# Three moves in the step plan of a linear-attention block: splits of the folded weight, one tile's statistics, one pair's feature maps

## The chip, the cores and the metric

The kernel runs on one core of a Trainium2 chip. The metric is the device time of one execution in microseconds; "before" is the median of three runs. The profile shows one execution of its own. The engines are named as the profile names them: PE (matmul; PEld is its weight load), DVE (VectorE), ACT (ScalarE), POOL (GpSimd) and SP, whose queue issues the transfers. Each works through its own instructions in the order in which the program issues them, and waits for others by semaphores.

## The reference

All numbers are 32-bit floats; S = 2048 rows, D = 576, H = 32 heads of 18, F = 4608.

```python
def _A_ref(x, wqkv, wo):
    qkv = (x @ wqkv).reshape(B, S, 3, H, Dh).transpose(2, 0, 3, 1, 4)
    q, k, v = qkv[0], qkv[1], qkv[2]
    phi = lambda t: jnp.where(t > 0, t + 1, jnp.exp(t)) + 1e-6
    pq, pk = phi(q), phi(k)
    kv = jnp.einsum("bhsd,bhse->bhde", pk, v)
    z = jnp.einsum("bhsd->bhd", pk)
    num = jnp.einsum("bhqd,bhde->bhqe", pq, kv)
    den = jnp.einsum("bhqd,bhd->bhq", pq, z)[..., None] + 1e-6
    o = num / den
    return o.transpose(0, 2, 1, 3).reshape(B, S, D) @ wo

xn = _layernorm(x)
s = _A_ref(xn, A_wqkv, A_wo)
g = _silu(gelu(xn @ w1 + b1) @ w2 + b2)
return x + s * g
```

## The kernel before, in words

Every matrix product is made from operands that are split in a high part (ACT casts it) and a low part (DVE or POOL subtracts), three matmuls for one. Most products also use a seven-product scheme on 2x2 blocks, so blocks of x and of the weights are added and subtracted first. There are three phases.

**Keys and values.** The 2048 rows are 16 tiles of 128, taken in eight pairs p = 0 to 7; `(p, s)` is tile s of pair p. Each tile is loaded (`load_x`, SP), its statistics are taken (`x_stats`, L237: five short instructions on DVE, then a power and a product on POOL), it is normalized on ACT (`x_norm`, L251), transposed by PE into the one PSUM tile `pt` (`transpose_x`, L266), and its parts are written (`x_hi`, `x_raw`, `x_lo`, `x_lo_tmp`, the block sums `x_sum` into `scr`, then `s_hi` on ACT and `s_lo`, L315, on DVE). `x_store` sends the parts to DRAM from SP's queue. Pair 0 is written out by hand (L530 to L586); for pairs 1 to 7 `plan_pair` (L600) puts calls into the table `plans` by step number, 14 steps (`NSP`) for a pair, and `at_step` issues a step's calls, in the order in which they were added, behind a piece of the pair's matmuls. Pair 1's keys are plain products (`Plain`); later pairs use `Proj`, whose second product `b` reads `xSL`, the low parts of the sums. The feature map of a key tile `ka` or `kb` is `phi_exp` (ACT), `phi_max` (L437, DVE) and `phi_add` (L440, ACT); the tiles then go into the state (`do_state`, PE, step 3 of the next pair) and into a running sum on POOL (`k_sum`). In pair 1 `wkq.sums` makes block sums of the key weight on POOL (L180), and `wkq.split_sums` splits them (L156 on ACT, L157 on DVE).

**Queries.** Rounds r = 0 to 9, again 14 steps each. Round 0 folds the attention state into the output weight (`fold_wo`, L771): PE writes 126-row blocks, which are copied to `kw`, and transfers from SP's queue (L794, L797) move their rows into tiles `kr` of 128 rows. `split_kw` (L767) makes the high part `kw_h` on ACT (L768) and the low part `kw_l` on DVE (L769) of one such tile. Splits 0 and 1 are issued in round 0 and at step 3 of round 1. In rounds 1 to 7 a `Proj` in the order `K_UP` = (1, 6, 7, 5, 2, 4, 3) makes the queries of a pair: product 1 goes to PSUM `a` and ACT copies it (L361); 6 and 7 are added up on DVE (L364, L367); 5 goes to `e`, and DVE adds it up (L357); 2 is accumulated onto `a`, which the copy must have read; 4 goes to `z` again, which L367 must have read; 3 is accumulated onto `e` behind L357. Behind it stand the exponentials and maxima of the queries, the denominators (`den_mul` POOL, `den_sum` DVE, `den_div` POOL), a padding copy on ACT (`pad`, L826), the transposes (`transpose_p`, `p_hi`, `p_lo`: L841, L845, L846) and from r = 2 on the attention product `Attend` (L866), which reads `kw_h` and `kw_l` of all five row blocks; `store` copies it from PSUM on ACT (L874).

**The gated feed-forward.** 18 steps over chunks of the hidden size, by a table of the same kind (`NS` = 28 steps each). `W2.hi` and `W2.lo` split the second weight's blocks; the first chunk's blocks are planned by `PW2` with one more entry.

What sets the order around the change is therefore the step number, and within a step the order of the `add` calls; all engines and SP's queue issue in that order.

Of the kernel before, what the change touches and what calls it, by code (L numbers as in the profile page):

```python
# [37 lines left out]
NSP = 14  # L38
# [4 lines left out]
def linear_attention_gated_ffn(ctx, tc, x, wqkv, wo, w1, b1, w2, b2, out):  # L43
    nc = tc.nc
# [91 lines left out]
    def pair_cols(p):  # L136
        return p % 4
# [99 lines left out]
    def x_stats(p, s, first=False):  # L237
        st = t1.tile([P, 2, 6], F32, tag="st", name=f"st{p}{s}")
        raw = xraw[p, s]
        nc.vector.bn_stats(st[:, 0, :], raw[:, :HD])  # L240
        nc.vector.bn_stats(st[:, 1, :], raw[:, HD:])
        mv = t1.tile([P, 4], F32, tag="mv", name=f"mv{p}{s}")
        nc.vector.bn_aggr(mv[:, 0:2], st)
        nc.vector.tensor_scalar_add(mv[:, 2:3], mv[:, 1:2], 1e-5)
        nc.gpsimd.tensor_tensor(mv[:, 3:4], mv[:, 2:3], nhalf, op=ALU.pow)
        if not first:
            nc.vector.tensor_scalar(mv[:, 0:1], mv[:, 0:1], -1.0, None, op0=MUL)
            nc.gpsimd.tensor_tensor(mv[:, 2:3], mv[:, 0:1], mv[:, 3:4], op=MUL)
        stats[p, s] = mv

    def x_norm(p, s, on_vector=False):  # L251
        mv, raw = stats.pop((p, s)), xraw.pop((p, s))
        t = xn[p, s] = t1.tile([P, 640], F32, tag="xn", name=f"xn{p}{s}")
        parts = (t[:, :D], raw), (t[:, D:], raw[:, 512:])
        if on_vector:
            for dst, src in parts:
                nc.vector.tensor_scalar(dst, src, mv[:, 0:1], mv[:, 3:4], op0=SUB, op1=MUL)
            return
        for dst, src in parts:
            nc.scalar.activation(dst, src, AF.Identity, scale=mv[:, 3:4], bias=mv[:, 2:3])  # L260
# [25 lines left out]
    def x_lo(p, s):  # L286
        cs, src = pair_cols(p), pts[p, s]
        tt = nc.vector.tensor_tensor
        if s == 0:
            tt(xL[:, 0:4, cs], src[:, :4], xH[:, 0:4, cs].bitcast(F32), op=SUB)  # L290
        else:
            tt(xL[:, 4:6, cs], src[:, 2:4], xH[:, 5:7, cs].bitcast(F32), op=SUB)
        r = xH[64:, 4 + 3 * s, cs]
        tt(r, src[64:, 4], r.bitcast(F32), op=SUB)
# [17 lines left out]
    def s_hi(p):  # L312
        nc.scalar.copy(xSH[:, :, pair_cols(p)], s_raw)

    def s_lo(p):  # L315
        cs = pair_cols(p)
        nc.vector.tensor_tensor(
            xSL[:, :, cs], s_raw[:, :8], xSH[:, :8, cs].bitcast(F32), op=SUB
        )
        r = xSH[64:, 8, cs]  # L320
        nc.vector.tensor_tensor(r, s_raw[64:, 8], r.bitcast(F32), op=SUB)

    def x_store(p):
        cs = pair_cols(p)
        for t, a, b in X_PARTS:
            nc.sync.dma_start(x_dram[p // 4][:, cs, a:b], t[:, :, cs].bitcast(F32))
# [180 lines left out]
    def add(step, fn, *args):  # L507
        plans.setdefault(step, []).append((fn, args))
# [64 lines left out]
    x_raw(1, 0)  # L573
    x_lo(1, 0)
    x_norm(1, 1)
    s_hi(0), s_lo(0)
    x_stats(2, 0)
    x_store(0)
    plain_v(0, 1).part(0, N14)
    phi_exp(k_t[1], e_t[1])  # L580
# [19 lines left out]
    def plan_pair(p):  # L600
        base = p * NSP
# [57 lines left out]
        ka, kb = k_ts[p % 2]  # L659
        ea, eb = e_t  # L660
        if p == 1:
            add(base + 3, phi_exp, ka, ea)
            add(base + 4, phi_max, ka, ea)
            add(base + 5, phi_add, ka)
            add(base + 11, k_sum, ka)
        else:
            add(base + 6, phi_exp, ka, ea)
            add(base + 7, phi_max, ka, ea)
            add(base + 7, phi_add, ka)
            add(base + 8, k_sum, ka)  # L670
        add(base + 7, phi_exp, kb, eb)
        add(base + 8, phi_max, kb, eb)
        add(base + 10, phi_add, kb)
        add(base + 12, k_sum, kb)
        for n, j in enumerate(W2_FIRST.get(p, ())):
            add(base + (1, 3)[n], w2_sum, j)
# [18 lines left out]
    for p in range(1, NPAIR):  # L695
        plan_pair(p)
        base = p * NSP
        if p > 1:
            pr = Proj(p, wkq, k_ts[p % 2], mu1)
            steps = [(pr.step, (i,)) for i in K_UP]  # L700
        else:
            pr = plain_k(p, 0)
            steps = [(pr.part, v) for v in ((0, 5), (5, 10), (10, 14))]
            steps += [(lambda a, b: cur.update(pr=plain_k(1, 1)) or cur["pr"].part(a, b), (0, 4))]
            steps += [(lambda a, b: cur["pr"].part(a, b), v) for v in ((4, 8), (8, 11), (11, 14))]
        for k, (fn, args) in enumerate(steps):
            fn(*args)
            at_step(base + k)
        for s in range(2):
            pr = plain_v(p, s)  # L710
            for k, v in enumerate(((0, 5), (5, 10), (10, 14))):
                pr.part(*v)
                at_step(base + 7 + 4 * s + k)
            if s == 0:
                at_step(base + 10)
# [18 lines left out]
    base = NPAIR * NSP  # L734
# [237 lines left out]
    for r in range(NPAIR + 2):  # L972
        base = (NPAIR + r) * NSP
# [20 lines left out]
        if 1 <= r < NPAIR:  # L994
            a, b = q_tiles(r)
            at = base + 2 * (r == 2)
# [4 lines left out]
            add(at + (8 if r > 1 else 14), phi_add, a)  # L1001
            add(at + (9 if r > 1 else 15), phi_add, b)
        if r == 1:
            add(base + 6, split_kw, 2, nc.vector)
            add(base + 8, split_kw, 3, nc.vector)
        if 1 <= r <= 6:
            add(base, w2_load, r + 2, *((w1p, "wa") if r % 2 == 0 else (w2rp, "w2raw")))
        if 2 <= r <= 7:
# [24 lines left out]
        if 1 <= r < NPAIR:  # L1033
            for s in range(2):
                at = Attend(r - 2, s) if r >= 2 else None
# [14 lines left out]
        elif r == NPAIR:  # L1050
            w = w1t[0]
            at = Attend(r - 2, 0)
# [6 lines left out]
            at = Attend(r - 2, 1)  # L1059
# [12 lines left out]
        elif r > NPAIR:  # L1072
            for s in range(2):
                at = Attend(r - 2, s)
# [328 lines left out]
    def plan_w1(add, w, base, T, hi, lo):  # L1403
        for table, what in ((T, w.T), (hi, w.hi), (lo, w.lo)):
            for i, at in table.items():
                add(base + at, what, i)
# [11 lines left out]


    PW2 = {1: 3, 7: 4, 3: 6}  # L1420
    W2_SUMS_NEXT = {5: 23, 6: 27}
    W2_SUMS_FIRST = {4: 4, 5: 6, 6: 10}
    W2_NEXT = {1: 15, 2: 17, 7: 19, 4: 21, 5: 23, 3: 25, 6: 27}
# [14 lines left out]
    w2t = {}  # L1438
# [5 lines left out]
    for step in range(n_chunks):  # L1444
        half, c = divmod(step, NC)
        base = step * NS
        plain = step == n_chunks - 1
        h = HOps(c)
        if half == 0:
            plan_w1(add, w1t[2 * step + 1], base, **P1)  # L1450
            if step == 0:
                add(base + 2, w2t[step].sum7)
            for i, at in PW2.items() if step else (*PW2.items(), (2, 5)):
                add(base + at, w2t[step].hi, i)
                add(base + at, w2t[step].lo, i)
            if step == 0:
                for i, at in W2_SUMS_FIRST.items():
                    add(at, w2t[0].load, i)
        if half == 0 and c < NC - 1:
# [11 lines left out]
            add(base + 25, nxt.lo, 4)  # L1471
            for i, at in W2_SUMS_NEXT.items():
                add(base + at, lambda i=i, n=step + 1: w2t[n].load(i))
# [102 lines left out]
```

## Time and profile before

| | |
|---|---|
| median of 3 runs | 1124.46 us (1124.1 to 1124.77) |
| the profiled execution | 1125.04 us, its span 1123.3 us |
| mean granted TensorE clock | 0.996 of full |
| PE busy | 1103.1 us, 98% of the span |
| DVE busy | 835.4 us, 74% |
| ACT busy | 506.4 us, 45% |
| POOL busy | 483.8 us, 43% |

The span is the time from the first to the last instruction of the one profiled execution; the times of the runs hold what lies around it too. Busy time is a mean over phases with different limits: PE's 98% come mostly from the feed-forward. In a row of the timeline stand start and duration in us, engine, line, operation, what is written and read, the shape, and in brackets the idle time of the engine just before and what ended it. In a row of waits stand the total in us, the number of waits and the longest. A row by stages has its start and end, its length, the busy time of PE, PEld, DVE, ACT and POOL with the number of instructions, the granted clock, the share of time in which the DMA engines were busy, and GB/s.

### The profile page before, as it was taken

Reading aid. Unit: us, or ns where it says so; the run is one execution under the profiler, and the core shown is the slowest. Engines: PE = TensorE matmul, PEld = TensorE weight load, DVE = VectorE, ACT = ScalarE, POOL = GpSimd, SP = SyncE. Lnnn points to the kernel's source line nnn. Section 1 sums busy time; section 2 is a strip of 40 time slices with the busy share of each in tenths; the row PEclk is TensorE's granted clock in tenths of the full one; section 3 lists DMA queues with packets and bytes.
Section 4 is the critical chain, followed back from the end, with each engine's and each line's share of the span. In section 5 each row is a group of like instructions: output and inputs, shape, how many; then the busy total and the mean of one; then the engine's idle time right before and its main releaser. Section 6 shows DMA issues by size and latency. Waiting matters only on the chain.

```text
span 1123.3 us, 18672 instructions
## 1 busy us (share of the span) xinstructions
PE 1103.1 (98%) x6924; PEld 1017.8 (91%) x6924; DVE 835.4 (74%) x1250; ACT 506.4 (45%) x913; POOL 483.8 (43%) x411
## 2 busy tenths in 40 slices
PE   8899998999999999999999999999999999999997
PEld 7899998999988988989989899898898998989987
DVE  5878766877598988989889898666475674764766
ACT  6756643555545454454544544524233242242352
POOL 5555334555364644646456444325234232242340
PEclk9999998999999999999999999999999999999999
DMA  5756536784978477485584849978666666766243
GB/s 201 270 210 240 222 99 203 259 295 153 352 280 332 144 274 263 167 321 179 231 295 159 319 157 366 390 249 266 221 199 222 210 207 209 230 200 222 87 130 125
DMA packets 89098, 257.16 MB, mean 229 GB/s; under 512 B 9581, under 2 KB 20333, under 8 KB 86959
## 3 DMA queue, kind: packets, MB, share of 16 engines
q1 hardware_dynamic: 89007, 255.96, 64.5%
q8 instruction: 55, 0.90, 0.3%
q14 instruction: 36, 0.29, 0.1%
HBM read 155.03 MB, written 100.01 MB: 227 GB/s over the span
## 4 chain that ended last, share of the span: by engine, by line
PE 81%; DVE 8%; ACT 4%; issue 3%; DMA 2%; POOL 2%; SPq 0%; DVEq 0%; POOLq 0%; ACTq 0%
PE pm L1255 32%; PE e L1118 11%; PE zy L1118 10%; PE a L1118 10%; PE b L1118 4%; PE pl L404 4%; PE ps_s L866 2%; PE pd L1372 2%; PE e L349 1%; DVE w2o L501 1%; PE z L349 1%; DMA kr<-kw 1%; DVE h_l L896 1%; PE ps_kva L457 1%; PE a L349 1%
## 5 line engine op out<-in xcount | busy, mean ns | idle before, releaser
L1262 DVE TENSOR_TENSOR macc<-pm,macc 128x576 f32<-128x576 f32 x218 | 164.1, 753 | 47.9 <-PE pm L1255 46.7
L893 ACT CAST h_h<-g 128x512 fp32r<-128x512 f32 x204 | 120.0, 621 | 142.2 <-PE pm L1255 141.1
L896 DVE TENSOR_TENSOR h_l<-g,h_h 128x512 fp32r<-128x512 f32 x204 | 171.3, 840 | 0.0
L1223 POOL TENSOR_TENSOR mid<-g 128x512 f32<-128x512 f32 x34 | 44.0, 1295 | 185.0 <-ACT g L1126 185.0
L1118 PE MATMUL a<-xH,wa 128*128 128x512 f32 x360 | 117.1, 390 | 0.0
L1118 PEld LDWEIGHTS a<-xH,wa 128*128 128x128 f32 x360 | 67.6, 188 | 13.6
L1126 ACT ACTIVATE g<-b,b1c 128x512 f32<-128x512 f32 x36 | 24.8, 690 | 121.5 <-DVE b L1144 121.5
L1118 PE MATMUL e<-xSH,wb 128*128 128x512 f32 x216 | 66.7, 390 | 0.9 <-DVE b L1144 0.9
L1343 POOL TENSOR_TENSOR fin1l<-fin1h,fin1l 128x288 f32<-128x288 f32 x8 | 6.5, 807 | 121.5 <-DMA fin1l<-s_dram 64.7
L1217 POOL TENSOR_TENSOR g<-g 128x512 f32<-128x512 f32 x34 | 49.5, 1457 | 20.8 <-DVE h_l L896 19.5
L1135 ACT COPY mid<-a 128x512 f32<-128x512 f32 x36 | 21.2, 588 | 78.4 <-PE a L1118 78.3
L1118 PE MATMUL a<-xL,wa 128*128 128x512 f32 x144 | 56.2, 391 | 0.0
L1220 POOL TENSOR_TENSOR g<-g 128x512 f32<-128x512 f32 x34 | 49.9, 1469 | 13.1 <-DVE h_l L896 11.7
L1214 POOL TENSOR_TENSOR g<-g 128x512 f32<-128x512 f32 x34 | 51.3, 1508 | 2.7
L1138 DVE TENSOR_TENSOR mid<-b,mid 128x512 f32<-128x512 f32 x36 | 24.6, 684 | 35.4 <-PE b L1118 35.3
L1118 PE MATMUL b<-xSH,w 128*128 128x512 f32 x144 | 50.2, 389 | 0.0
L1118 PE MATMUL zy<-xSH,w 128*128 128x512 f32 x144 | 50.2, 389 | 0.0
L1118 PE MATMUL e<-xSH,w 128*128 128x512 f32 x144 | 50.2, 389 | 0.0
L1118 PE MATMUL zy<-xH,w 128*128 128x512 f32 x144 | 50.2, 389 | 0.0
L1118 PEld LDWEIGHTS e<-xSH,wb 128*128 128x128 f32 x216 | 40.6, 188 | 10.1 <-DVE b L1144 1.8
L896 DVE TENSOR_TENSOR h_l<-mid,h_h 128x512 fp32r<-128x512 f32 x34 | 43.1, 1268 | 6.0 <-ACT h_h L893 6.0
L1126 ACT ACTIVATE g<-e,b1c 128x512 f32<-128x512 f32 x36 | 24.8, 690 | 48.8 <-DVE e L1151 48.8
(928 smaller groups left out, 3589.2 us busy)
## 6 DMA issues: line engine op xcount, KB each, us to landing
op<-w SPq DMA_DIRECT2D x72, 256.0 KB
w<-op SPq DMA_DIRECT2D x72, 256.0 KB
w1raw<-w SPq DMA_DIRECT2D x18, 640.0 KB
w2raw<-w SPq DMA_DIRECT2D x10, 1152.0 KB
op_a<-wa SPq DMA_DIRECT2D x18, 640.0 KB
wa<-op_a SPq DMA_DIRECT2D x18, 640.0 KB
op<-w2o SPq DMA_DIRECT2D x19, 576.0 KB
w2r<-w SPq DMA_DIRECT2D x6, 1152.0 KB
```

The source lines that it names most:

```text
L349: nc.tensor.matmul(ps, st, mv, start=first and n == 0, stop=n == len(seq) - 1, skip_group_check=True,)
L404: nc.tensor.matmul(self.ps[n], st, self.wk(hl, k, n), start=(i == 0), stop=(i == n_all - 1))
L893: nc.scalar.copy(pair[0], src)
L896: eng.tensor_tensor(pair[1], src, pair[0].bitcast(F32), op=SUB)
L1118: nc.tensor.matmul(ps.rearrange("p (c j) -> p c j", c=4), st, mv, start=first and n == 0, stop=n == len(seq) - 1, skip_group_check=True,)
L1126: nc.scalar.activation(g, ps, AF.Gelu_apprx_tanh, bias=b1c[:, f : f + 1])
L1214: tt(src[5, pr], A(1, 0), A(1, 1), op=ADD)
L1217: tt(src[6, pr], src[5, pr], A(0, 0), op=SUB)
L1220: tt(src[3, pr], A(0, 1), src[6, pr], op=SUB)
L1223: tt(src[7, pr], A(0, 0), A(1, 0), op=SUB)
L1255: nc.tensor.matmul(ps[:, q, :HD], hs[p][st][:, cs], m[:, p, :], start=(n == 0 and i not in CHAIN), stop=(n == len(seq) - 1), skip_group_ch ...
L1262: nc.vector.tensor_tensor(dst, src, dst, op=ADD)
```

## The change

Three groups of calls are moved; no call is added or left out. The statistics of tile (2, 0), the fifth to be normalized, are issued ahead of `s_hi(0)` and `s_lo(0)`. In pair 1 the first key tile's `phi_max` goes from step 4 to 6 and its `phi_add` from 5 to 9; the second tile's `phi_add` from 10 to 11. In round 1 `split_kw(2)` goes from step 6 to 12, and `split_kw(3)` from step 8 to step 2 of round 2. The table `PW2_FIRST` holds the same entries as the expression that it replaces, and the calls stand at the same steps.

```diff
@@ -573,8 +573,8 @@
     x_norm(1, 1)
+    x_stats(2, 0)
     s_hi(0), s_lo(0)
-    x_stats(2, 0)
     x_store(0)
@@ -660,8 +660,8 @@
         if p == 1:
             add(base + 3, phi_exp, ka, ea)
-            add(base + 4, phi_max, ka, ea)
-            add(base + 5, phi_add, ka)
+            add(base + 6, phi_max, ka, ea)
+            add(base + 9, phi_add, ka)
             add(base + 11, k_sum, ka)
@@ -670,7 +670,7 @@
         add(base + 8, phi_max, kb, eb)
-        add(base + 10, phi_add, kb)
+        add(base + (11 if p == 1 else 10), phi_add, kb)
         add(base + 12, k_sum, kb)
@@ -1001,8 +1001,8 @@
         if r == 1:
-            add(base + 6, split_kw, 2, nc.vector)
-            add(base + 8, split_kw, 3, nc.vector)
+            add(base + 12, split_kw, 2, nc.vector)
+            add(base + NSP + 2, split_kw, 3, nc.vector)
@@ -1418,6 +1418,7 @@
     PW2 = {1: 3, 7: 4, 3: 6}
+    PW2_FIRST = {1: 3, 7: 4, 2: 5, 3: 6}
@@ -1448,11 +1449,12 @@
-            for i, at in PW2.items() if step else (*PW2.items(), (2, 5)):
-                add(base + at, w2t[step].hi, i)
-                add(base + at, w2t[step].lo, i)
+            w2c = w2t[step]
...
+            for i, at in (PW2 if step else PW2_FIRST).items():
+                add(base + at, w2c.hi, i)
+                add(base + at, w2c.lo, i)
```

More of the change, by code (lines that the diff above doesn't have):

```diff
@@ L1450, in linear_attention_gated_ffn @@
             plan_w1(add, w1t[2 * step + 1], base, **P1)
-            if step == 0:
-                add(base + 2, w2t[step].sum7)
-            for i, at in PW2.items() if step else (*PW2.items(), (2, 5)):
-                add(base + at, w2t[step].hi, i)
-                add(base + at, w2t[step].lo, i)
+            w2c = w2t[step]
+            if not step:
+                add(base + 2, w2c.sum7)
+            for i, at in (PW2 if step else PW2_FIRST).items():
+                add(base + at, w2c.hi, i)
+                add(base + at, w2c.lo, i)
             if step == 0:
```

## The prediction

> **What bounds the kernel now.** I read the page first: its span and the granted clock in 40 slices.
>
> ```profile
> span 1123.3 us, 18672 instructions
> ...
> PEclk9999998999999999999999999999999999999999
> ```
>
> The reader is to see that one slice of 28.1 us (the seventh, 168 to 197 us) ran below full clock, and that it is the slice in which the moved splits of the folded weight stand. Next, what TensorE waited for, over the whole span:
>
> ```profile
> PE a L349 <- ACT scr L361: 2.6, 1, 2.6
> ...
> PE pt L270 <- DVE scr L310: 1.6, 1, 1.6
> PE pt L270 <- ACT wkq_h L156: 1.3, 1, 1.3
> ```
>
> All three lie in the steps the change edits: the 2.6 us at r = 2 of the query rounds, the other two in pair p = 1. Third, the chain of work that ended last.
>
> ```profile
> 70.50 0.80 PE b L349 x4
> ...
> 161.05 1.06 PE a L349 x8
> ...
> 164.24 6.33 PE ps_kw L783 x24
> 170.93 11.43 DMA kr<-kw
> ```
>
> From 70.50 to 164.24 the chain has rows of PE alone, so whatever pair 1 wins or loses by 70 us arrives whole at 164 us. Then it follows a row transfer for 11.43 us, to 182.4 us. Fourth, ACT in order of time behind that transfer, and PE beside it.
>
> ```profile
> 182.44 0.67 ACT L768 CAST kw_h<-kr 128x576 fp32r<-128x576 f32 x1 [4.07 <-DMA kr<-kw]
> 183.01 0.77 ACT L435 ACTIVATE e<-scr,c 128x576 f32<-128x576 f32 x1
> ...
> 184.36 0.66 ACT L768 CAST kw_h<-kr 128x576 fp32r<-128x576 f32 x1
> 184.92 0.39 ACT L361 COPY scr<-a 128x288 f32<-128x288 f32 x1
> ```
>
> ```profile
> 182.50 0.29 PE L349 MATMUL e<-wkq_rl,xH 128*128 128x288 f32 x1
> 185.36 0.61 PE L349 MATMUL a<-wkq_h,xH 128*128 128x288 f32 x1 [2.57 <-ACT scr L361]
> ...
> 191.74 0.54 PE L866 MATMUL ps_s<-kw_h,th 128*128 128x288 f32 x2
> ```
>
> ACT runs its queue in order. It sits 4.07 us on split 2, whose rows are in flight; behind it wait two exponentials, split 3 and the copy of `a` (L361), and PE needs that copy before it may add onto `a`: 2.57 us without work. By stages, the clock:
>
> ```profile
> 31.50:35.00 3.50, 1.93 (x17) 1.73 (x16) 3.42 (x9) 1.89 (x3) 2.18 (x4) 1.00 1.01 346
> ...
> 181.70:185.10 3.40, 1.09 (x9) 0.85 (x7) 1.96 (x3) 2.66 (x5) 0.00 (x0) 1.00 0.35 96
> 185.10:188.50 3.40, 3.05 (x11) 2.71 (x12) 3.22 (x8) 2.65 (x5) 1.85 (x2) 0.51 0.98 406
> 188.50:192.00 3.50, 3.50 (x17) 3.50 (x16) 3.20 (x6) 0.24 (x1) 2.90 (x3) 0.50 1.02 411
> ```
>
> The first figures are PE's busy time, the third from the end the clock. Behind a stretch with PE busy 1.09 of 3.40 us the clock is half for 6.9 us; behind one with 1.93 of 3.50 (the 1.6 us wait above) it stays full. So the 2.57 us wait is paid twice.
>
> **Part 1: the query rounds.** Split 2 moves from step 6 to 12 of r = 1, split 3 to step 2 of r = 2. No instruction is added and no DMA is moved; the transfers start where they did, so I let split 2's rows land at 182.44. What is new is the order on ACT: the two exponentials (inputs ready, nothing else on ACT in the 4.07 us) now run inside the wait, then split 2, then the copy. The copy starts at 182.44 + 0.57 (the step from the split to the next start) = 183.01 instead of 184.92. PE's wait shrinks to about 183.45 - 182.79 = 0.7 us. The wait for the rows is not removed; two exponentials and split 3, 1.9 us, leave the path behind it. Queued behind split 2 are now the copy, a cast and two adds on ACT, and PE waits for the copy: each us by which the rows land later is lost one for one. Split 3 found its rows at 184.36 without a wait and asks for them at 185.2, behind the adds: no new wait. What is late next stands on DVE:
>
> ```profile
> 183.14 0.76 DVE L769 TENSOR_TENSOR kw_l<-kr,kw_h 128x576 fp32r<-128x576 f32 x1 [3.40 <-ACT kw_h L768]
> ...
> 185.83 0.45 DVE L364 TENSOR_TENSOR scr<-b,scr 128x288 f32<-128x288 f32 x1
> 186.20 0.68 DVE L845 TENSOR_TENSOR tl<-ptp,th 128x512 fp32r<-128x512 f32 x1
> ...
> 187.22 0.46 DVE L367 TENSOR_TENSOR scr<-z,scr 128x288 f32<-128x288 f32 x1
> 187.81 0.46 DVE L357 SCALAR_TENSOR_TENSOR rt<-e,scr 128x288 f32<-128x288 f32 x1
> ```
>
> The low part of split 2 keeps 183.14; the two maxima go ahead of it into the 3.40 us, split 3's low part behind L367. So L364 starts at 183.8 (2.0 earlier), L367 at 185.2 and ends at 185.7. PE's accumulation onto `a`, 8 matmuls, takes 1.06 us at full clock (the chain's row at 161.05) and ends near 184.5; `z` then waits 1.2 us for L367, runs to 186.8, and `e` waits for L357, now behind split 3's low part (ACT high part 185.2 to 185.9, DVE 186.0 to 186.7): 187.1 to 188.2. The attention product starts near 188.2 instead of 191.74, 3.5 us earlier: half is the wait, half the clock. It lasts 3.8 us as before (191.74 to the copy that waits for it at 195.65, less the start of a copy) and ends near 192.0. That copy out of PSUM comes behind the second pad on ACT:
>
> ```profile
> 194.38 0.25 ACT L826 COPY pbuf<-pbuf 128x64 f32<-128x64 f32 x1 [2.90 <-POOL pbuf L817]
> 195.65 0.70 ACT L874 COPY s<-ps_s 128x288 f32<-128x288 f32 x2 [1.02 <-PE ps_s L866]
> ```
>
> The pad hangs on denominators (DVE, then POOL), which follow the `e` add on DVE; that add gains only about 1.0 (187.81 to 186.8). POOL's products before them follow ACT's adds behind the copy, 1.9 us earlier, and so overlap DVE's sums less. Between 1.0 and 1.9 I put the pad at 1.5, 192.9. The copy then runs at 193.05, behind the pad and no longer behind PE: **2.6 us** earlier. Bounds: 1.5 if the following rounds go by the pad, 3.5 if they go by PE. I take the copy, since the next casts and exponentials stand behind it on ACT. Later rounds wait on engines, not on transfers:
>
> ```profile
> ACT pbuf L826 <- POOL pbuf L817: 16.8, 10, 2.6
> ```
>
> so they move as a block, and the PE-bound rest behind them too.
>
> The Trainium skill (TensorE: Matmul & The Clock Gate, Part 1: The HAM clock gate) says the clock falls to half after at least one idle window of about 3.4 us. Here 2.57 us without work was enough, so the measurement decides; by the page the shorter waits left over could not trip it and the sum stands, by the row they might, and that is the first rival.
>
> **Part 2: the fifth tile's statistics.** They move ahead of the first pair's low parts.
>
> ```profile
> 28.53 1.23 DVE L317 TENSOR_TENSOR xSL<-scr,xSH 128x1024 fp32r<-128x1024 f32 x1 [1.20 <-ACT xSH L313]
> ...
> 30.09 0.47 DVE L240 BATCH_NORM_STATS2 st<-x 128x6 f32<-128x288 f32 x1
> ...
> 31.44 0.42 DVE L298 TENSOR_TENSOR x_tmp1l<-pt,x_tmp1h 128x256 fp32r<-128x256 f32 x1
> ```
>
> ```profile
> 29.93 0.41 ACT L281 CAST x_tmp1h<-pt 128x256 fp32r<-128x256 f32 x1
> 32.35 1.20 ACT L260 ACTIVATE xn<-x,mv 128x576 f32<-128x576 f32 x2 [2.00 <-POOL mv L248]
> ```
>
> ```profile
> 28.00:30.00 2.00, 2.00 (x18) 2.00 (x17) 1.46 (x2) 2.00 (x6) 0.00 (x0) 1.00 0.00 0
> ```
>
> The statistics take 31.44 - 30.09 = 1.35 us and fit DVE's idle 1.20 before L317; their tile has landed, as DMA moves nothing here (the last column). L317 starts 0.15 late, with it the stores and two loads that SP queues behind it; their tiles are read 8 us later, which covers that. L298 then waits for ACT's cast (30.34) instead of the statistics: 30.4, **1.0 us** earlier, and with it the sums that free the PSUM tile of the 1.6 us wait. The normalization, which waited 2.00 us for these statistics, is out of the way as well.
>
> **Part 3: pair 1's feature maps.**
>
> ```profile
> 41.08 1.58 DVE L438 SCALAR_TENSOR_TENSOR k<-e,k 128x576 f32<-128x576 f32 x1
> 42.59 1.21 DVE L317 TENSOR_TENSOR xSL<-scr,xSH 128x1024 fp32r<-128x1024 f32 x1
> ...
> 46.49 3.55 DVE L157 TENSOR_TENSOR wkq_l<-wt,wkq_h 128x1152 fp32r<-128x1152 f32 x2 [0.16 <-ACT wkq_h L156]
> 49.96 0.75 DVE L438 SCALAR_TENSOR_TENSOR k<-e,k 128x576 f32<-128x576 f32 x1
> 50.63 1.21 DVE L317 TENSOR_TENSOR xSL<-scr,xSH 128x1024 fp32r<-128x1024 f32 x1
> ```
>
> ```profile
> 40.61 1.44 POOL L180 TENSOR_TENSOR wt<-raw,wt 128x576 f32<-128x576 f32 x1
> ```
>
> The maximum took 1.58 us beside POOL's L180 and 0.75 alone: it started only when L180 ended at 42.0. Taken out, it does not give back its 1.5 us, because L317 meets the same L180 (1 us earlier by part 2): it runs from 41.0 instead of 42.6, so 0.6 beyond part 2. ACT's wait for this maximum goes too, and the weight casts come 1.4 earlier. But the maximum returns between the two L157: + 0.67 (50.63 - 49.96, the step of its twin). The second L317, on which PE's `b` of pair 2 waits, is earlier by 1.4 - 0.7 = **0.7 us**, and so is everything to 164 us. Bounds: 1.6 if POOL costs nothing in either place, and a loss of 0.2 if the maximum pays its 1.58 at the new place too. I take 0.67, as POOL's two sums there already lie inside the 3.55.
>
> The Trainium skill (GPSIMD Engine Reference, section 1, Specifications) has GpSimd's SBUF interface shared with VectorE instructions of two SBUF inputs; the 1.58 agrees, and by it alone the price at the new place would be the upper one, part 3 a loss of 0.2 and the forecast 1122.1.
>
> `PW2_FIRST` gives the old steps: nothing.
>
> **Sum.** 0.7 + 2.6 = 3.3 us off the span of 1123.3. The execution around it took 1125.04, and the median of the runs is 1124.46: I subtract from the median, **1121.2 us**.
>
> **Rivals.** (a) The clock falls once more. The waits left (0.7 and 1.2 us, 1.06 of work between) make 1.9 in 3 us, between the two stretches quoted. At half clock from 185.9 for 6.9 us, `z` and `e` end at 189.9; until 192.8 the attention product gets through 1.5 of its 3.8 us and ends near 195.1, the copy at 195.2: 0.45 earlier; with part 3 1.15: **1123.3**. For it, 2.57 was enough; against it, work lies between, and the windows must fall together.
>
> (b) More than forecast: rounds follow PE (3.5) and pair 1 gains 1.6: 5.1, **1119.4**. The pad's 1.5 speaks against.
>
> (c) The gain is absorbed where weights stream before the main loop, or the rows land later by what ACT saves (the change then does not do what it says): **1124.4**. Against it: no row transfer is issued elsewhere, and the rounds wait on engines.
>
> (d) Slower: half clock over more stretches of 3.4 us than before. With three, the attention product ends at 196.8, its copy 1.2 later than now, less 0.7: **1125.0**; each further one adds some 1.5. It decides from the third on. Against it: PE is busy throughout from 188 us.
>
> **Numbers.** Forecast 0.56, (a) 0.16, (b) 0.13, (c) 0.07, (d) 0.08. A difference of 0.2%, 2.2 us, is what a measurement can tell from none. Faster: forecast, (b) and a little of (a), 0.70; slower half of (d) and some unforeseen queue, 0.06; the rest 0.24. The range runs from between (b) and its bound to just above (a): 1119.2 to 1123.7.
>
> **What would show it.** PE's wait for L361 under 1 us, two exponentials ahead of the `kr` cast in ACT's order, and a clock of 1.00 from 185 to 192 us; PE's `z` waiting over 1 us for L367; the transposes of pair 1 waiting under 1 us. Wrong if the clock row still shows half, or if the 11.43 us of the transfer grow.

## The result and the profile after

The changed kernel took 1121.15 us (median of 9 runs, 1120.46 to 1124.37); the kernel before, beside it, 1124.77 us (9 runs, 1123.73 to 1125.18). The medians lie 3.6 us apart. The ratio is 0.9971, with a 95% interval from 0.9961 to 0.9981, that is 3.3 us faster, 2.1 to 4.4 by the interval. The forecast was 1121.2 us.

The page of the changed kernel, its span and the granted clock in 40 slices:

```profile
span 1118.8 us, 18673 instructions
...
PEclk9999999999999999999999999999999999999999
```

The seventh slice is at full clock now. What TensorE waited for, over the whole span of the changed kernel (total in us, number of waits, the longest):

```profile
PE z L349 <- DVE scr L367: 1.5, 2, 0.9
PE pt L270 <- DVE scr L310: 1.1, 2, 0.6
PE b L349 <- DVE xSL L317: 1.0, 2, 0.6
...
PE a L349 <- ACT scr L361: 0.9, 1, 0.9
```

The 2.6 us for L361 are 0.9, the 1.6 for L310 and the 1.3 for L156 have given way to waits of 0.6 each. To see where the 4.5 us of the span came from, the stages of the two profiled executions are laid side by side. First the kernel before, then the changed one; each row runs from the first pair's sum (L313) to the first product of the fold (L783), or from there to the first attention product (L866). Third from the end stands the clock.

```profile
27.27:164.07 136.80, 132.92 (x1032) 131.07 (x1032) 103.76 (x207) 83.31 (x152) 64.39 (x67) 1.00 0.58 214
164.07:191.74 27.67, 24.35 (x136) 20.89 (x135) 20.04 (x40) 13.61 (x28) 9.59 (x8) 0.88 0.52 173
```

```profile
26.78:162.50 135.72, 132.99 (x1032) 131.06 (x1032) 103.30 (x207) 83.34 (x152) 65.27 (x67) 1.00 0.59 216
162.50:187.04 24.54, 21.92 (x137) 18.34 (x136) 18.53 (x37) 13.37 (x27) 8.42 (x6) 1.00 0.46 140
```

The keys and values are 1.1 us shorter, the stretch from the fold to the first attention product 3.1. The same stages in every profiled execution follow, in us. In this table the fold of the changed kernel starts at 162.53, where the trace has it, and not at the 162.50 of the rows above. L874 is the copy that follows the attention product, and L1118 the first product of the feed-forward.

| profiled execution | L313 starts | L313 to L783 | L783 to L866 | L783 to L874 | L866 to L1118 | L1118 to the end | span |
|---|---|---|---|---|---|---|---|
| before | 27.27 | 136.80 | 27.67 | 31.58 | 103.66 | 827.9 | 1123.3 |
| after | 26.78 | 135.75 | 24.51 | 28.67 | 103.79 | 827.9 | 1118.8 |
| e1_splits | 26.75 | 136.78 | 24.44 | 28.57 | 103.78 | 828.0 | 1119.7 |
| e2_stats | 29.23 | 135.73 | 27.91 | 32.23 | 104.05 | 827.9 | 1124.8 |
| e3_maps | 26.96 | 136.77 | 27.55 | 31.35 | 103.54 | 828.0 | 1122.8 |
| e4_fill | 26.72 | 136.76 | 26.18 | 30.14 | 103.61 | 827.5 | 1120.8 |
| e5_late | 27.21 | 135.76 | 22.11 | 28.80 | 106.33 | 827.7 | 1119.1 |
| e6_split3_front | 29.79 | 135.78 | 24.81 | 28.88 | 103.77 | 828.0 | 1122.1 |
| e7_late_stats | 27.19 | 135.74 | 22.08 | 28.76 | 106.30 | 827.8 | 1119.1 |
| e8_late_sums | 27.87 | 135.71 | 21.91 | 28.17 | 106.05 | 827.9 | 1119.5 |
| e9_sums | 28.97 | 135.71 | 25.63 | 29.43 | 103.49 | 827.9 | 1121.7 |
| e10_after | 27.16 | 135.67 | 24.40 | 28.54 | 103.74 | 827.9 | 1118.9 |
| e11_fill_sums | 26.73 | 135.73 | 24.44 | 28.23 | 103.46 | 827.5 | 1117.8 |

From before to after: -1.05 in the keys and values, -3.16 from the fold to the attention product (-2.91 to its copy), +0.1 in the rest, and -0.5 at the start. That last term isn't the change's: the start lies between 26.7 and 29.8 us from execution to execution, also where nothing ahead of it differs (26.78 and 27.16 in two executions of the changed kernel). The three latest starts, 28.97 to 29.79 us in e2, e6 and e9, are those of the three executions whose clock had fallen to half near 9 us; the other ten lie between 26.7 and 27.9. A single span can therefore be 2 to 3 us off without a reason in the edit, and stages are the better measure.

The queries, ACT and then TensorE in order of time (start, duration, instruction, in brackets the idle time before it and what ended that):

```profile
178.31 0.78 ACT L435 ACTIVATE e<-scr,c 128x576 f32<-128x576 f32 x1 [1.47 <-DVE scr L357]
179.00 0.76 ACT L435 ACTIVATE scr<-scr,c 128x576 f32<-128x576 f32 x1
181.10 0.67 ACT L768 CAST kw_h<-kr 128x576 fp32r<-128x576 f32 x1 [1.34 <-DMA kr<-kw]
181.68 0.39 ACT L361 COPY scr<-a 128x288 f32<-128x288 f32 x1
...
191.05 0.25 ACT L826 COPY pbuf<-pbuf 128x64 f32<-128x64 f32 x1 [2.27 <-POOL pbuf L817]
191.20 0.69 ACT L874 COPY s<-ps_s 128x288 f32<-128x288 f32 x2
```

```profile
182.12 0.40 PE L349 MATMUL a<-wkq_h,xH 128*128 128x288 f32 x1 [0.86 <-ACT scr L361]
...
184.38 0.40 PE L349 MATMUL z<-wkq_h,xH 128*128 128x288 f32 x1 [0.92 <-DVE scr L367]
```

Both exponentials run ahead of split 2, whose wait for its rows is 1.34 us instead of 4.07, and the copy of `a` follows it at once. TensorE waits 0.86 us for that copy and 0.92 for L367. The copy L874 starts on the end of the second pad, 191.05 + 0.25, give or take the overlap of two starts: it stands behind the pad, no longer behind TensorE. The margin is small, as TensorE's part of the product that the copy reads had ended at 190.92. The transfer is the old one, 0.2 us longer than the 11.43 of before, in the chain of work that ended last:

```profile
169.41 11.61 DMA kr<-kw
```

### The profile page after: what moved, and what is told of

The parts are those of the page before. It is cut to its first block, busy times and chain, and to the rows that moved or that the text cites. A ratio compares the mean times of both kernels' runs of the same rounds, so it can differ in the third digit from the quotient of the medians.

```text
span 1118.8 us, 18673 instructions
## 1 busy us (share of the span) xinstructions
PE 1099.8 (98%) x6924; PEld 1014.6 (91%) x6924; DVE 834.3 (75%) x1250; ACT 506.2 (45%) x913; POOL 485.2 (43%) x411
## 4 chain that ended last, share of the span: by engine, by line
PE 82%; DVE 7%; ACT 4%; issue 2%; DMA 2%; POOL 2%; SPq 0%; DVEq 0%; POOLq 0%; ACTq 0%
PE pm L1255 32%; PE e L1118 12%; PE zy L1118 10%; PE a L1118 10%; PE b L1118 4%; PE pl L404 4%; PE ps_s L866 2%; PE pd L1372 2%; PE e L349 1%; DVE w2o L501 1%; DMA kr<-kw 1%; DVE h_l L896 1%; PE z L349 1%; PE ps_kva L457 1%; PE a L349 1%
## 5 line engine op out<-in xcount | busy, mean ns | idle before, releaser
L1118 PE MATMUL a<-xH,wa 128*128 128x512 f32 x360 | 117.1, 390 | 0.0
L1118 PEld LDWEIGHTS a<-xH,wa 128*128 128x128 f32 x360 | 67.6, 188 | 13.6
L1118 PE MATMUL e<-xSH,wb 128*128 128x512 f32 x216 | 66.8, 390 | 0.9 <-DVE b L1144 0.9
L1118 PE MATMUL a<-xL,wa 128*128 128x512 f32 x144 | 56.2, 390 | 0.0
L1118 PE MATMUL b<-xSH,w 128*128 128x512 f32 x144 | 50.2, 389 | 0.0
L1118 PE MATMUL zy<-xH,w 128*128 128x512 f32 x144 | 50.2, 389 | 0.0
L1118 PE MATMUL zy<-xSH,w 128*128 128x512 f32 x144 | 50.2, 389 | 0.0
L1118 PE MATMUL e<-xSH,w 128*128 128x512 f32 x144 | 50.2, 389 | 0.0
L1118 PEld LDWEIGHTS e<-xSH,wb 128*128 128x128 f32 x216 | 40.5, 188 | 10.1 <-DVE b L1144 1.7
```

The costliest lines, as they stand in the source:

```text
L1118: nc.tensor.matmul(ps.rearrange("p (c j) -> p c j", c=4), st, mv, start=first and n == 0, stop=n == len(seq) - 1, skip_group_check=True,)
```

## The experiments

Times are medians with their range; each ratio is against the kernel before on the same chip, with its 95% interval. The first four runs shared a chip, as did e5 to e7, e8 and e9, e10 and e11.

### One part at a time: e1, e2, e3

The kernel before, with the splits moved alone:

```diff
-            add(base + 6, split_kw, 2, nc.vector)
-            add(base + 8, split_kw, 3, nc.vector)
+            add(base + 12, split_kw, 2, nc.vector)
+            add(base + NSP + 2, split_kw, 3, nc.vector)
```

> Only the two moves of the folded weight's splits, on the kernel before. Theory (the sum by stages): the stage from the fold products (L783) to the first attention product (L866) falls from 27.7 us to about 24.5, as in the changed kernel, and the first stage stays at 136.8 us from the first pair's s_hi to L783; the median is some 3 us below before (about 1121.8). Rival (the parts need each other): the stage falls by less than 2 us and the median by less than 1.5.

Measured: 1121.91 us (1121.27 to 1123.98, 10 runs), ratio 0.9976 (0.9967 to 0.9985). From the fold to the attention product -3.23 us and to its copy -3.01, with nothing in the stage before it (-0.02). The splits carry the whole of that stage's gain.

With the statistics alone:

```diff
+    x_stats(2, 0)
     s_hi(0), s_lo(0)
-    x_stats(2, 0)
```

> Only the statistics moved, on the kernel before. Theory: they alone bring the first stage (s_hi of pair 0 to L783) from 136.8 to about 135.8 us, because everything behind them, also the blocked maximum at 41 us, moves by 1.0; the median falls by 1.0 (1123.8). Rival (the prediction's way of counting, by which the maximum's move has a part in it): 0.4 us or less is left without the feature maps' move.

Measured: 1124.13 us (1123.48 to 1126.54, 11 runs), ratio 0.9992 (0.9983 to 1.0001). The interval touches 1, so the runs alone don't settle it; the stage does: 135.73 us against 136.80, -1.07. TensorE's waits in this kernel:

```profile
PE pt L270 <- ACT wkq_h L156: 1.3, 1, 1.3
...
PE pt L270 <- DVE scr L310: 0.5, 1, 0.5
```

The wait for L310 went from 1.6 to 0.5 and the one for L156 stayed: all of it is the tile freed earlier. Its profiled execution started 2 us late and had two stretches at half clock, so its span isn't to be compared.

With the feature maps alone:

```diff
-            add(base + 4, phi_max, ka, ea)
-            add(base + 5, phi_add, ka)
+            add(base + 6, phi_max, ka, ea)
+            add(base + 9, phi_add, ka)
...
-        add(base + 10, phi_add, kb)
+        add(base + (11 if p == 1 else 10), phi_add, kb)
```

> Only pair 1's feature maps moved, on the kernel before. Theory: nothing within 0.3 us in the first stage (136.8), since the maximum's 1.5 us ahead of the low parts are taken over by the low parts' own wait for the same POOL instruction and its return between the weight splits costs 0.3 to 0.7; the median stays at 1124.8. Rival: 0.6 us or more is gained, or 0.7 lost.

Measured: 1125.12 us (1124.18 to 1129.82, 11 runs), ratio 1.0004 (0.9993 to 1.0015); the stage 136.77 against 136.80. Nothing. Why, stands in ACT and DVE of this kernel, whose stage starts 0.31 us earlier than that of the kernel before:

```profile
43.53 1.20 ACT L260 ACTIVATE xn<-x,mv 128x576 f32<-128x576 f32 x2 [1.61 <-POOL mv L248]
44.64 2.19 ACT L156 CAST wkq_h<-wt 128x1152 fp32r<-128x1152 f32 x2
```

```profile
40.77 2.05 DVE L317 TENSOR_TENSOR xSL<-scr,xSH 128x1024 fp32r<-128x1024 f32 x1
...
45.88 1.36 DVE L157 TENSOR_TENSOR wkq_l<-wt,wkq_h 128x1152 fp32r<-128x1152 f32 x1 [0.53 <-ACT wkq_h L156]
47.16 1.29 DVE L438 SCALAR_TENSOR_TENSOR k<-e,k 128x576 f32<-128x576 f32 x1
48.38 1.35 DVE L157 TENSOR_TENSOR wkq_l<-wt,wkq_h 128x1152 fp32r<-128x1152 f32 x1
...
50.31 1.22 DVE L317 TENSOR_TENSOR xSL<-scr,xSH 128x1024 fp32r<-128x1024 f32 x1
```

ACT no longer waits for the maximum, but between its exponential and the weight casts (L156) stands a normalization (L260), and that waits 1.61 us for the statistics on POOL (L248). These come behind L180 and a power (L245), which takes 1.54 us beside the low parts there. DVE loses the maximum's 1.5 us (42.59 - 41.08), gives 0.8 of it back (L317 beside L180 took 2.05 us instead of 1.21) and then waits 0.53 for those casts. Its first L157, at 45.88 instead of 46.49, is 0.3 ahead once the earlier start is taken off, and the maximum between the two L157 takes that back: from the first L157 to the second maximum it is 3.77 us, against 3.47 before (49.96 - 46.49). The second L317 starts at 50.31 instead of 50.63: the 0.31 of the start, and nothing more. On TensorE it reads as two waits of 0.6 us that take the place of the one of 1.3 for L156:

```profile
PE pt L270 <- DVE scr L310: 2.2, 2, 1.6
PE b L349 <- DVE xSL L317: 1.0, 2, 0.6
```

### The clock by itself: e4

The kernel before with its order and its wait for the rows, and 18 transposes into an unused PSUM tile put where TensorE stands still (their results are not used):

```diff
+                if (r, k) == (2, 4):
+                    idle = psS.tile([P, 512], F32, tag="p1", name="idle")
+                    for _ in range(18):
+                        nc.tensor.transpose(idle[:, :P], ident, ident)
```

> The kernel before, with 18 transposes into a spare PSUM tile on PE ahead of product 2 of round 2, inside the wait for the copy of a; they add PE work of some 2 us and compute nothing that is used. The order of all other instructions and the wait for the rows stay. Theory (the wait is paid twice, once by the clock): the clock stays at 1.00 from 185 to 192 us, product a still starts at its old place behind the copy, but the attention product starts about 1.8 us earlier and its copy about 1.2 earlier; the median falls by about 1.2 (1123.6). Rival (the clock does not matter because DVE and POOL set the pace there): the median stays within 0.4.

Measured: 1122.72 us (1122.33 to 1124.49, 11 runs), ratio 0.9983 (0.9974 to 0.9992); the attention product 1.49 us earlier than in the kernel before, its copy 1.44, at full clock.

```profile
182.07 2.12 PE L1030 MATMUL idle<-ident 128*128 128x128 f32 x18
185.07 0.40 PE L349 MATMUL a<-wkq_h,xH 128*128 128x288 f32 x1 [0.87 <-ACT scr L361]
```

Nothing but TensorE's idleness was changed, so the wait was paid twice, as the prediction had it. Of the 3.16 us some 1.5 are clock, and the other 1.7 are the wait that fell from 2.57 to 0.86. The 1.5 is rather too low: split 2's rows landed 0.3 us later behind the fold here than in the kernel before (18.66 us against 18.37), which without that would make some 1.8, as expected; in the changed kernel they landed 0.2 later (18.57). The median fell by 2.5 us on this chip, more than the stage gives: in the trace another 0.5 lies in the start and 0.4 in the feed-forward, neither of which the edit touches.

### Still later: e5, e7

The changed kernel, with split 2 and 3 behind the round's own adds (e5); the same with the feature maps at their old places (e7):

```diff
-            add(base + 12, split_kw, 2, nc.vector)
-            add(base + NSP + 2, split_kw, 3, nc.vector)
+            add(base + NSP + 3, split_kw, 2, nc.vector)
+            add(base + NSP + 5, split_kw, 3, nc.vector)
```

> The changed kernel with split 2 at step 3 and split 3 at step 5 of round 2, so that the copy of a stands ahead of both on ACT. Theory (what is left of the stage is the copy behind the rows): PE's 0.9 us wait for the copy is gone, L364 and L367 come some 1.5 to 2 us earlier, the stage from L783 to the first attention product falls from 24.5 to about 22.5 us and the median from 1121.2 to about 1119.2. Rival (the denominators on DVE and POOL set the pace from here, the pad being the last before the copy out of PSUM): the stage falls, but the copy out of PSUM comes less than 1 us earlier and the median stays above 1120.2.

> As the late placing of both splits, with the statistics moved and the feature maps at their old steps. Theory (the feature maps' move is worth nothing also beside the others): the first stage (s_hi of pair 0 to L783) is 135.75 us as in the changed kernel, the median within 0.4 us of the late placing with the feature maps moved. Rival: the first stage is 0.4 us or more longer than in the changed kernel, as the feature maps' move shortens it once the statistics are out of the way.

Measured: e5 1120.81 us (1120.4 to 1121.27, 5 runs), ratio 0.9967 (0.9954 to 0.9979); e7 1120.78 us (1120.34 to 1121.41, 6 runs), 0.9966 (0.9954 to 0.9978). In e5 the attention product starts 2.4 us earlier than in the changed kernel (22.11 against 24.51), and the part of it that the copy reads ends 1.5 earlier, as it waits 0.67 us for a low part on its way. The copy behind it comes not at all earlier (28.80 against 28.67). That is the rival's outcome. DVE, POOL and ACT of e5:

```profile
183.31 1.99 DVE L769 TENSOR_TENSOR kw_l<-kr,kw_h 128x576 fp32r<-128x576 f32 x1
...
186.80 1.73 DVE L769 TENSOR_TENSOR kw_l<-kr,kw_h 128x576 fp32r<-128x576 f32 x1
```

```profile
183.27 1.42 POOL L804 TENSOR_TENSOR scr<-scr,zb 128x576 f32<-128x576 f32 x1
186.74 1.18 POOL L817 TENSOR_TENSOR pbuf<-scr,den 128x576 f32<-128x576 f32 x1 [2.05 <-DVE den L814]
```

```profile
191.62 0.24 ACT L826 COPY pbuf<-pbuf 128x64 f32<-128x64 f32 x1 [3.42 <-POOL pbuf L817]
191.77 0.69 ACT L874 COPY s<-ps_s 128x288 f32<-128x288 f32 x2
```

Each low part (0.76 us by itself) starts beside a product on POOL and ends 0.6 us after that: 1.99 and 1.73 us. DVE's sums for the denominators stand behind them, then POOL's division, then the pad, then the copy. So in e5 the round goes by the pad. It says less of the changed kernel, as the low parts that were moved now stand in the pad's own path; there the pad and TensorE are nearly level (end of the section on the result, and e11 below). And e7's first stage is 135.74 us, e5's 135.76: the feature maps are worth nothing beside the other parts either.

### Split 3 back ahead of the copy: e6

The changed kernel, with `split_kw(3)` at step 12 of round 1, behind split 2:

```diff
-            add(base + NSP + 2, split_kw, 3, nc.vector)
+            add(base + 12, split_kw, 3, nc.vector)
```

> The changed kernel with split 3 back ahead of the copy of a (step 12 of round 1, behind split 2). Theory: one more high part on ACT (0.57) and one more low part on DVE (0.67) ahead of the copy and of L364: PE's wait for the copy grows from 0.9 to about 1.4 us, the stage from 24.5 to about 24.9, as the low part no longer stands behind L367 ahead of the sum e waits for; the median is up by 0.3 to 0.7, more in runs where the longer wait halves the clock. Rival (only split 2's place counts): no change within 0.2.

Measured: 1123.47 us (1120.7 to 1124.94, 11 runs), ratio 0.9983 (0.9972 to 0.9994). In the profiled execution TensorE waits 1.6 us for the copy, and the attention product comes only 0.30 us later than in the changed kernel, at full clock. Yet 8 of the 11 runs took 1122.26 to 1124.94 us with a mean clock of 0.995 to 0.997, and three 1120.7 to 1121.12 with 0.999 to 1.0: most runs lost clock, and the others did not. The median is 2.3 us above the changed kernel's 1121.15, measured on another chip; 0.3 to 0.7 was expected, and more in runs that lose clock. The profiled execution of 1123.93 us lost its clock elsewhere, from 9.5 to 12.9 us (below), so where the other seven lost it isn't shown.

### POOL's product out of the way, and the wait filled: e8 to e11

Round 2 runs two of POOL's products for the second weight (L492) at steps 4 and 5, ahead of its divisions; e8 is e5 with these at 6 and 7, e9 the changed kernel with them there. e10 is the changed kernel again, and e11 is e9 with six transposes into an unused tile ahead of TensorE's products at steps 4 and 5, as in e4.

```diff
-                add(base + ((0, 3) if r > 2 else (4, 5))[j], w2_sum, n + j)
+                add(base + ((0, 3) if r > 2 else (6, 7))[j], w2_sum, n + j)
...
+                if (r, k) in ((2, 4), (2, 5)):
+                    idle = psS.tile([P, 512], F32, tag="p1", name=f"idle{k}")
+                    for _ in range(6):
+                        nc.tensor.transpose(idle[:, :P], ident, ident)
```

> The late placing of both splits (steps 3 and 5 of round 2), and in round 2 POOL's two sums of the second weight (L492) at steps 6 and 7 instead of 4 and 5, behind the denominators' products. Theory (in the late placing the pad before the copy out of PSUM hangs on POOL's sum, 1.9 us ahead of the second product, and on DVE's low parts that wait for it): from L783 to the copy falls from 28.8 to about 27.4 us and the median from 1120.8 to about 1119.4. Rival (the copy is held by the low parts on DVE alone): less than 0.4 us.

> The changed kernel with only these two POOL sums moved to steps 6 and 7. Theory (there PE's attention product ends at the same moment as the pad, so both would have to come earlier): the copy out of PSUM comes at most 0.3 us earlier (28.67 us behind L783), the median stays within 0.4 of 1121.2. Rival (the pad alone holds it): 1 us earlier.

> The changed kernel as it is, beside the next one on the same chip. Theory (the two waits left halve the clock in some executions): most runs lie at 1120.4 to 1121.3 with a mean clock of 0.999 to 1.0, and some, about one in five, at 0.997 or below and 1 to 4 us longer. Rival: the long runs of the first measurement were chance, and all runs lie within 1 us.

> The changed kernel with POOL's two sums of round 2 at steps 6 and 7, and six transposes into a spare PSUM tile on PE in each of the two waits left in round 2 (ahead of products 2 and 4; they compute nothing that is used). Theory: PE has no wait over 0.4 us there, the clock stays at 1.00 in every run's stage, no run lies over 1 us above the median, and the median is 0.2 to 0.8 us below the changed kernel's on the same chip. Rival (the halved clock has nothing to do with these waits): as many long runs as the changed kernel has.

Measured: e8 1120.52 us (1119.99 to 1121.2, 5 runs), ratio 0.9958 (0.9946 to 0.9971); its copy 28.17 us behind the fold's start, 0.63 earlier than e5's, between the 1.4 of the theory and the rival's 0.4. Its low parts still take 2.02 and 1.72 us, beside L804 and L817, so the move frees the division and not DVE. e9 1120.34 us (1120.09 to 1123.44, 5 runs), 0.9957 (0.9943 to 0.997); its profiled execution is the one of 1123.44, at half clock from 186.6 to 190.0 us, so it doesn't show what the move does to the copy at full clock. e10 1120.59 us (1120.2 to 1120.82, 5 runs), 0.9957 (0.9944 to 0.9969), without a long run among the five. That is what the rival said; but if one run in five loses clock, five runs without a loss still come in a third of such trials, so it decides little. e11 on the same chip 1119.58 us (1119.53 to 1121.77, 5 runs), 0.9953 (0.994 to 0.9967). Four of its runs lie within 0.25 us, some 1.0 below the changed kernel's; against the kernel before the two intervals overlap. The fifth took 2.2 us more, which the filled waits were to prevent: one long run of five against none of e10's, so the runs don't bear out this part of the theory. Nor is the 1.0 all the edit's: between the profiled executions of e10 and e11 the copy moves by 0.3, and the start and the feed-forward, which the edit leaves as they are, differ by 0.4 each. In e11 the copy waits for TensorE again:

```profile
190.69 0.70 ACT L874 COPY s<-ps_s 128x288 f32<-128x288 f32 x2 [0.30 <-PE ps_s L866]
```

So where the pad comes earlier, at full clock, the copy follows by 0.3 us and then stands behind TensorE: in the changed kernel the pad is last, but only just.

### When the clock falls

In all 13 profiled executions the clock changes on a grid of 3.41 us, and it also falls at the end, when TensorE has run out of work. Counted back from there, every window of that grid can be read for its TensorE time, whether the clock fell behind it or not. Windows of the kernel before (two places), of e9 and of e6, each with the window behind it. The first figure behind the length is TensorE's work, the third from the end the clock:

```profile
31.55:34.96 3.41, 1.84 (x15) 1.64 (x14) 3.33 (x9) 1.85 (x3) 2.09 (x4) 1.00 1.00 341
34.96:38.38 3.42, 3.42 (x32) 3.42 (x31) 0.47 (x4) 2.91 (x6) 3.25 (x5) 1.00 1.07 357
...
181.74:185.15 3.41, 1.05 (x8) 0.81 (x7) 2.01 (x3) 2.71 (x5) 0.00 (x0) 1.00 0.36 100
185.15:188.56 3.41, 3.11 (x11) 2.77 (x12) 3.23 (x8) 2.60 (x5) 1.91 (x2) 0.50 0.98 406
```

```profile
183.19:186.60 3.41, 1.58 (x11) 1.14 (x9) 2.48 (x5) 3.33 (x6) 1.01 (x1) 1.00 0.56 184
186.60:190.01 3.41, 3.41 (x14) 3.41 (x15) 3.17 (x7) 0.54 (x2) 2.81 (x3) 0.50 0.97 399
```

```profile
183.61:187.02 3.41, 1.85 (x14) 1.58 (x12) 2.23 (x5) 2.82 (x6) 0.00 (x0) 1.00 0.44 125
187.02:190.44 3.42, 2.49 (x19) 2.29 (x18) 3.17 (x8) 1.14 (x3) 2.79 (x2) 1.00 0.99 409
```

The lowest work behind which the clock stayed is 1.84 us, in the first row above and in a window near 30 us of e3 and of e4, with e6's 1.85 next. The highest behind which it fell is in e2:

```profile
6.30:9.71 3.41, 1.76 (x9) 1.13 (x9) 3.38 (x5) 1.47 (x3) 2.66 (x2) 1.00 1.01 372
9.71:13.12 3.41, 3.27 (x13) 3.28 (x14) 2.61 (x8) 1.19 (x2) 2.78 (x3) 0.50 1.05 401
```

The seven falls ahead of the end come behind 0.72, 1.05, 1.07, 1.46, 1.58, 1.60 and 1.76 us of work in 3.41 (windows between 4 and 16 us and between 178 and 192 us), and those at the end behind 1.23 us or less. No full-clock window of the 13 executions with 1.84 or more is followed by a fall, and none with 1.76 or less goes without one. So what counts here isn't the longest wait but the work in a window of the grid, and the limit, in TensorE time as this profile counts it, lies between 1.76 and 1.84 us, about half. Where the grid lies differs with each execution. In the changed kernel it parted the two waits:

```profile
179.33:182.75 3.42, 2.56 (x19) 2.33 (x18) 2.17 (x4) 2.08 (x5) 0.00 (x0) 1.00 0.17 60
182.75:186.16 3.41, 2.33 (x16) 1.86 (x15) 3.10 (x7) 2.21 (x4) 2.74 (x2) 1.00 0.95 346
181.00:184.41 3.41, 1.63 (x12) 1.17 (x10) 2.47 (x5) 3.31 (x6) 0.99 (x1) 1.00 0.57 177
```

The first two rows are its grid; the third is the worst place that a window could have, and would have been too low. With a window laid every 0.1 us and 1.8 us taken as the limit, the share of grid positions at which the clock would fall in the query stage is 28 of 34 for the kernel before, 14 of 34 for e6, 7 of 34 for e4 and e9, 6 of 34 for e1 and the changed kernel, and none for e5, e7, e8 and e11, whose lowest windows hold 2.71 to 2.96 us; each count is good to about one place. This agrees with the runs as far as these tell. Of the runs of the kernel before beside e1 to e11, 58 of 66 had a mean clock of 0.997 or less. So had two of the changed kernel's 14 (1121.69 and 1124.37 us), two of e1's 10, three of e4's 11 (1124.17 to 1124.49), two of e9's 5, none of the 16 of e5, e7 and e8 nor of e11's 5, and 8 of e6's 11, which is more than its share. A run without a profile doesn't tell where its clock fell, and the windows of the first 10 us, in which the work waits for the inputs (ACT 4.8 us for the transfer of the weight in e6), can trip it too (e2, e6, e9). That e11's one long run fell there isn't shown; its mean clock of 0.998 tells little, as two of e7's runs had it at their usual time.

## Why the prediction was right

**What bounds the kernel.** Right. The order on ACT behind a transfer in flight was the cause (e1), and the wait was paid a second time in the clock (e4).

**Part 1.** The mechanism is right in each step that was named: exponentials, split 2, copy; 0.86 us for the copy where 0.7 was forecast, 0.92 for L367 where it was 1.2, the attention product at full clock. It started 24.5 us behind the fold where the working gave 24.1 (188.2 less 164.07), so 3.2 us were gained there and not 3.5. The step that chose between the bounds, the copy behind the pad and so 2.6 us, is right by the rows of the changed kernel, but only just: the forecast had TensorE's product end 0.9 us ahead of the pad (192.0 and 192.9), and it ended 0.1 ahead (190.92 and 191.05). That much of the choice was luck. As a size it was 0.3 too small: the pad came 28.5 us behind the fold, where the estimate between DVE's 1.0 and POOL's 1.9 gave 28.8 (192.9 less 164.07), and the copy gained 2.9.

**Part 2.** Right: 1.0 forecast, 1.07 measured in e2. DVE of the changed kernel:

```profile
28.17 1.22 DVE L317 TENSOR_TENSOR xSL<-scr,xSH 128x1024 fp32r<-128x1024 f32 x1
...
29.89 0.42 DVE L298 TENSOR_TENSOR x_tmp1l<-pt,x_tmp1h 128x256 fp32r<-128x256 f32 x1 [0.18 <-ACT x_tmp1h L281]
...
44.65 1.36 DVE L157 TENSOR_TENSOR wkq_l<-wt,wkq_h 128x1152 fp32r<-128x1152 f32 x1 [0.55 <-ACT wkq_h L156]
45.93 1.29 DVE L438 SCALAR_TENSOR_TENSOR k<-e,k 128x576 f32<-128x576 f32 x1
47.14 1.34 DVE L157 TENSOR_TENSOR wkq_l<-wt,wkq_h 128x1152 fp32r<-128x1152 f32 x1
...
49.08 1.21 DVE L317 TENSOR_TENSOR xSL<-scr,xSH 128x1024 fp32r<-128x1024 f32 x1
```

From the start of the sum's L313 (26.78, before 27.27) it is 1.39 us to L317 and 3.11 to L298; before it was 1.26 and 4.17. So the one is 0.13 us late (0.15 forecast), the other 1.06 early and waiting for ACT's cast, as forecast.

**Part 3.** Up to 164 us the forecast was 0.7 gained, made of parts 2 and 3 together; measured 1.05. The first half of the working is right: the first L157 and the casts it waits for came 1.35 us earlier (46.49 - 44.65, less the 0.49 of the start), where 1.4 was forecast. The failed step is the maximum's return, "+ 0.67": the second L317 came 1.06 earlier (50.63 - 49.08, less 0.49), so the return cost 0.29, as in e3. The 0.67 was the step of its twin, on the ground that POOL's two sums lie inside the 3.55 us of the L157 already. POOL's sums, before and after:

```profile
46.28 2.54 POOL L310 TENSOR_TENSOR scr<-scr 128x256 f32<-128x256 f32 x2 [2.42 <-DVE scr L310]
```

```profile
44.05 2.55 POOL L310 TENSOR_TENSOR scr<-scr 128x256 f32<-128x256 f32 x2 [1.78 <-DVE scr L310]
```

Before, both sums held DVE up, one L157 each: they took 1.74 and 1.89 us. In the changed kernel DVE waits 0.55 us for the cast instead of 0.16, so the first L157 begins 0.6 us behind the first sum instead of 0.2 and takes 1.36; the second sum holds up the maximum, 1.29 us instead of 0.75, and the second L157 takes 1.34. One of the two hold-ups, some 0.4 us, is gone, and 0.67 less that is the 0.29. Counted from the end of DVE's own sums ahead of the L157, the return did cost 0.67: DVE was free 1.74 us earlier there, and the second L317 came 1.06 earlier. By the forecast the maps would have cost 0.3 of part 2's 1.0; they cost nothing and gain nothing. Both given bounds, 1.6 and a loss of 0.2, hold the measured value. The loss of 0.2, with the maximum at its full 1.58, did not come. The sharing that the Trainium skill states (GPSIMD Engine Reference, section 1, Specifications) is there in the rows all the same, 1.29 us against 0.75.

**Sum.** 1.05 + 2.9 = 4.0 us in the stages where 3.3 were forecast, and 3.6 between the medians (3.3 by the ratio, 2.1 to 4.4). That the median met the forecast to 0.1 us is partly chance: an undersized sum, subtracted from a median of before of 1124.46 that came out at 1124.77 this time, and a median over runs of which some lose clock.

**Rivals.** (a), the clock falling once more, is real: e9's profiled execution, whose splits and waits are the changed kernel's (0.9 and 0.9 us), had it, and its attention product came at 25.63 instead of 24.51. No profiled execution of the changed kernel itself had it; its two long runs suggest it. Its price was put too high: the half clock lasted 3.4 us in e9, not 6.9, and the copy came 0.8 us later than in the changed kernel (29.43 against 28.67), where the working had 2.15 (195.2 less 193.05). The working put (a) as one outcome for all runs, with 0.16; it is a share of the runs, by the grid 6 in 34. The argument against it, that work lies between the waits, is not a bar: work between counts by its length, 1.06 us, and two waits of 0.9 with it leave 1.6 of 3.41. The Trainium skill's rule (TensorE: Matmul & The Clock Gate, Part 1: The HAM clock gate) has the right length of window, but not the idle window: 1.76 us of work didn't keep the clock. (b) came true in neither part; (c) is out, as the transfer took 11.61 us, only 0.2 more, and later rounds moved as a block (103.79 against 103.66); (d), three half-clock stretches, was seen in no profiled execution's query stage.

`PW2_FIRST` was costed at nothing, and the feed-forward took 827.9 us in both kernels.

## What to carry to other kernels

A wait in an in-order queue costs what stands behind it, so look there before looking at the transfer: here two exponentials with their inputs ready stood behind rows in flight, and moving them ahead gained 3 us, clock included, with the transfer as long as before to 0.2 us. A short wait of TensorE can be paid a second time in the clock, here 1.5 us for a wait of 2.57; measure its work over windows of the clock's own length at every phase, and move or fill work until none of them is below the limit. Where an engine's wait is taken away, go down its queue to the next instruction that waits for something else: the smaller of the two reliefs is all that one gets.

## What the hardware showed

The clock fell to half behind windows of 3.41 us with 1.76 us of TensorE work or less, and never behind 1.84 or more, on a grid that lies elsewhere in each execution. Of the changed kernel's runs, the two with a mean clock of 0.997 or less took 0.5 and 3.2 us more than the median. A VectorE instruction with two inputs in SBUF that began while such a POOL instruction ran lasted until that had ended, and then for its own time less 0.1 to 0.2 us: 1.99 instead of 0.76 us (L769), 2.05 instead of 1.21 (L317). And the start of the first stage varied by 3 us between executions of kernels that are equal up to there, the three latest being those that lost clock near 9 us.
